# A single-core attention and two-layer feed-forward kernel: other SBUF addresses for all its tiles, the same instructions

## The chip, the cores and the metric

One Trainium2 chip, one of its cores. The metric is the device time of one execution in microseconds (us), as the median of several executions. The chip's engines are named as in the profile: PE does matmuls, PEld is PE's weight load, DVE, ACT and POOL are the vector, scalar and GpSimd engines, SP issues the transfers.

## The reference

Clustered attention, whose output goes through two feed-forward blocks. There are 2 x 8 heads of 768 positions and 64 dimensions; 1536 tokens of 512 numbers go into the blocks, each 512 to 2048 to 512.

```python
q_assign = np.argmax(np.einsum('bhsd,hcd->bhsc', q_n, c_n), axis=-1)   # q_n, k_n, c_n: normalised
k_assign = np.argmax(np.einsum('bhsd,hcd->bhsc', k_n, c_n), axis=-1)
mask = q_assign[:, :, :, None] == k_assign[:, :, None, :]
scores = np.where(mask, scale * np.matmul(q, k.transpose(0, 1, 3, 2)), -1000000000.0)
attn = np.exp(scores - np.max(scores, axis=-1, keepdims=True))
attn = attn / (np.sum(attn, axis=-1, keepdims=True) + 1e-09)
x = np.matmul(attn, v)                      # then to [tokens, heads x dims]
...
h = x @ w_in;  x = np.maximum(0.01 * h, h) @ w_out              # first block
h = x @ w_in2; r = np.maximum(h, 0.0); x = (r * r) @ w_out2     # second block
```

## The kernel before

Every fp32 operand is split into a high and a low part, and three products (high x high, high x low, low x high) stand for one fp32 product. So PE runs many matmuls on 4-byte numbers.

**Attention.** Eight pairs of heads, 48 units of two query blocks of 128 rows. A unit makes its scores on PE (`S`, line 353, 384 columns, both operands in tile `hb`), the row maximum on DVE (`nm`), the exponentials on ACT (`e`), the division on POOL, twelve transposes on PE (`T`, line 416, stationary `e`, moving the identity matrix `ident`), the split of the transposes on ACT and DVE (`eh`, `el`), and the product with V on PE (`A`, line 451, 256 columns, moving `eh` or `el`, stationary `vv`). The order of all engines is written out by hand (table PLAN).

**Feed-forward blocks.** 16 blocks of hidden units in each of the two layers, three blocks of 512 tokens: 96 units. A unit is twelve matmuls of 512 columns into `h` (line 728, stationary `wh` or `wl`, moving `xh` or `xl`) and twelve into `o` (line 770; in the first layer the weights are stationary and `gh`, `gl` move, in the second layer `gh`, `gl` are stationary and the weights move). That makes 2304 matmuls of 512 columns. The weights arrive as raw 8-byte numbers in `wraw` and are decoded by ACT, DVE and POOL (lines 131 to 160) into `wh` and `wl` while PE works on the group before.

**Where the weights lie.** Hidden blocks are worked off in groups of four (the first four in two groups of two), and the weight tiles are a ring of eight: blocks 0 to 3 of every eight lie in pool `wpx`, which is allocated from the right end of SBUF, blocks 4 to 7 in pool `wpb`, on the left. So PE works for about 66 us with weights from `wpx`, then for about 65 us with weights from `wpb`, and so on, four stretches of each.

```python
wpx = ctx.enter_context(tc.tile_pool(name="wpx", bufs=G, side="right", reuse_waits="tile"))
ring.append((ctx.enter_context(tc.tile_pool(name="wpb", bufs=RING - G, reuse_waits="tile")), RING))
pool = next(q for q, n in ring if ci % RING < n)      # ci: the hidden block's number
```

**Addresses.** Pools are laid out one after the other, those of the left side upwards behind the DMA scratch, those with `side="right"` downwards from 229344 bytes in each partition. In the built program of before:

| tile (pool) | start in its partition, bytes | past a multiple of 512 | past a multiple of 128 |
|---|---|---|---|
| `ident` (const) | 16512 | 128 | 0 |
| `xh`, `xl` (xp) | 21600, 46176 | 96 | 96 |
| `hb`, `vv`, `e`, `eh`, `el`, `gh`, `gl`, `acc` and the other large tiles of the left side | 70752 and up | 96 | 96 |
| `wh`, `wl` (wpb, left) | 99424 to 128096, in steps of 4096 | 96 | 96 |
| `wh`, `wl` (wpx, right) | 184288 to 212960, in steps of 4096 | 480 | 96 |
| `rqk`, `spl`, `rv` (right, in the attention alone) | 189408 and up | 480 | 96 |

PE's operands are slices of these tiles at multiples of 512 bytes, so a slice has its tile's remainder (the 32-column `cbd` in `S` excepted).

Of the kernel before, what the change touches and what calls it, by code (L numbers as in the profile page):

```python
# [8 lines left out]
F32 = mybir.dt.float32  # L9
# [43 lines left out]
def attention_moe_moe_kernel(  # L53
# [9 lines left out]
    nc = tc.nc  # L63
# [17 lines left out]
    WARM = (9,4,10)  # L81

    const = ctx.enter_context(tc.tile_pool(name="const", bufs=1))
    xp = ctx.enter_context(tc.tile_pool(name="xp", bufs=1))

    xh = xp.tile([128, HP, NT], F32R, name="xh")
    xl = xp.tile([128, HP, NT], F32R, name="xl")
# [590 lines left out]
    for u in range(-1, NU + 5):  # L678
# [8 lines left out]
        for op in PLAN[FIRST[u] if p == 0 else u % UPP].split():  # L687
            if ":" in op:
                name, lag = op.split(":")
# [5 lines left out]
            else:  # L695
                name, ahead = op.split("@")
# [184 lines left out]
```

## Time and profile before

| what | value |
|---|---|
| time, median of 3 executions (lowest to highest) | 786.04 us (784.79 to 786.47) |
| the profiled execution's own time from its first to its last instruction (span) | 782.9 us |
| PE busy, of the span | 770.1 us (98%), 4147 matmuls |
| DVE, ACT, POOL busy | 532.2, 410.8, 293.4 us |
| attention: S, T and A matmuls | 384, 576 and 576 |
| feed-forward: matmuls into h and into o, 512 columns each | 1152 and 1152 |
| data moved by DMA | 66.35 MB, mean 85 GB/s |

The profile takes one execution. Its span is 3.1 us less than the median of the timed executions. A matmul's duration in the profile is its latency: matmuls overlap, so the pace of PE is read from the start of one piece of work to the start of the next, not from the durations.

### The profile page before, as it was taken

Reading aid. Unit: us, or ns where it says so; the run is one execution under the profiler, and the core shown is the slowest. Engines: PE = TensorE matmul, PEld = TensorE weight load, DVE = VectorE, ACT = ScalarE, POOL = GpSimd, SP = SyncE. Lnnn points to the kernel's source line nnn. Section 1 sums busy time; section 2 is a strip of 40 time slices with the busy share of each in tenths; the row PEclk is TensorE's granted clock in tenths of the full one; section 3 lists DMA queues with packets and bytes.
Section 4 is the critical chain, followed back from the end, with each engine's and each line's share of the span. In section 5 each row is a group of like instructions: output and inputs, shape, how many; then the busy total and the mean of one; then the engine's idle time right before and its main releaser. Section 6 shows DMA issues by size and latency. Waiting matters only on the chain.

```text
span 782.9 us, 11015 instructions
## 1 busy us (share of the span) xinstructions
PE 770.1 (98%) x4147; PEld 665.3 (85%) x4147; DVE 532.2 (68%) x772; ACT 410.8 (52%) x759; POOL 293.4 (37%) x258
## 2 busy tenths in 40 slices
PE   8999999999999999999999999999999999999998
PEld 8899999999988888888888888888888888888886
DVE  5899999999998568775664577487257557533333
ACT  6988988988997563443442343445344234212121
POOL 2989889889765412221220214442022012100000
PEclk9999999999999999999999999999999999999999
DMA  7594574573502223233121113013113103000102
GB/s 224 121 205 110 105 180 108 113 164 78 139 1 93 96 85 108 105 107 108 55 107 54 33 75 108 1 54 108 55 54 108 54 0 108 1 0 1 52 17 95
DMA packets 16005, 66.35 MB, mean 85 GB/s; under 512 B 2704, under 2 KB 2704, under 8 KB 10960
## 3 DMA queue, kind: packets, MB, share of 16 engines
q1 hardware_dynamic: 15952, 65.64, 29.2%
q8 instruction: 33, 0.54, 0.3%
q14 instruction: 20, 0.16, 0.1%
HBM read 44.60 MB, written 3.15 MB: 61 GB/s over the span
## 4 chain that ended last, share of the span: by engine, by line
PE 82%; DVE 12%; ACT 4%; issue 1%; POOL 0%; DVEq 0%; ACTq 0%; POOLq 0%
PE o L770 34%; PE h L728 33%; PE A L451 5%; PE S L353 4%; DVE el L433 4%; PE T L416 4%; DVE nm L376 4%; ACT e L386 2%; DVE xt L473 1%; ACT eh L427 1%; DVE ds L279 1%; PE warm L202 1%; PE ohT L308 1%; DVE m L278 1%; PE S L257 1%
## 5 line engine op out<-in xcount | busy, mean ns | idle before, releaser
L160 POOL TENSOR_TENSOR wl<-wt,wh 128x1024 fp32r<-128x1024 f32 x32 | 77.5, 2423 | 297.1 <-ACT wh L159 246.6
L728 PE MATMUL h<-xl,wh 128*128 128x512 f32 x384 | 150.6, 392 | 0.0
L728 PE MATMUL h<-xh,wl 128*128 128x512 f32 x384 | 150.5, 392 | 0.0
L728 PE MATMUL h<-xh,wh 128*128 128x512 f32 x384 | 150.4, 393 | 0.0
L749 DVE TENSOR_TENSOR gl<-g,gh 128x512 fp32r<-128x512 f32 x96 | 91.6, 954 | 44.1 <-ACT gh L748 44.0
L748 ACT CAST gh<-g 128x512 fp32r<-128x512 f32 x96 | 59.6, 621 | 80.5 <-DVE g L745 42.2
L433 DVE TENSOR_TENSOR el<-T,eh 128x512 fp32r<-128x512 f32 x144 | 94.4, 683 | 5.6 <-ACT eh L427 3.7
L403 POOL TENSOR_SCALAR e<-e,r 128x768 f32<-128x768 f32 x96 | 88.5, 933 | 20.7 <-DVE r L400 13.4
L376 DVE TENSOR_REDUCE nm<-S 128x1 f32<-128x768 f32 x96 | 90.8, 947 | 4.6 <-PE S L257 2.3
L386 ACT ACTIVATE e<-S,nm 128x768 f32<-128x768 f32 x96 | 87.0, 906 | 11.1 <-DVE nm L376 6.8
L353 PE MATMUL S<-hb 128*128 128x384 f32 (+1 forms) x384 | 90.5, 350 | 1.6 <-ACT e L386 1.2
L745 DVE TENSOR_TENSOR g<-t 128x512 f32<-128x512 f32 x48 | 39.5, 822 | 73.3 <-ACT t L744 73.2
L744 ACT ACTIVATE t<-h 128x512 f32<-128x512 f32 x48 | 28.7, 598 | 113.3 <-PE h L728 113.2
L728 PEld LDWEIGHTS h<-xh,wl 128*128 128x128 f32 x384 | 72.3, 188 | 16.1
L728 PEld LDWEIGHTS h<-xl,wh 128*128 128x128 f32 x384 | 72.2, 188 | 16.0
L728 PEld LDWEIGHTS h<-xh,wh 128*128 128x128 f32 x384 | 72.2, 188 | 15.9
L427 ACT CAST eh<-T 128x512 fp32r<-128x512 f32 x144 | 79.4, 586 | 10.6 <-PE T L416 10.2
L451 PE MATMUL A<-eh,vv 128*128 128x256 f32 x288 | 79.5, 307 | 3.0 <-DVE xt L473 3.0
L416 PE MATMUL T<-ident,e 128*128 128x128 f32 x576 | 80.0, 274 | 1.1 <-DVE el L433 1.0
L770 PE MATMUL o<-gh,wl 128*128 128x512 f32 x192 | 75.4, 393 | 0.0
L770 PE MATMUL o<-gl,wh 128*128 128x512 f32 x192 | 75.3, 392 | 0.0
L770 PE MATMUL o<-wh,gl 128*128 128x512 f32 x192 | 75.3, 392 | 0.0
(106 smaller groups left out, 1407.0 us busy)
## 6 DMA issues: line engine op xcount, KB each, us to landing
wraw<-w SPq DMA_DIRECT2D x32, 1024.0 KB, 4.7
hb<-spl SPq DMA_DIRECT2D x14, 576.0 KB, 4.8
hb<-spl SPq DMA_DIRECT2D x42, 192.0 KB, 5.1
rqk<-qk SPq DMA_DIRECT2D x16, 384.0 KB, 4.5
rv<-v SPq DMA_DIRECT2D x8, 384.0 KB, 4.1
out<-ob SPq DMA_DIRECT2D x12, 256.0 KB, 2.1
twice<-qk SPq DMA_DIRECT2D x8, 192.0 KB, 6.0
hb<-st SPq DMA_DIRECT2D x28, 48.0 KB, 2.7
```

Of the source, the lines that this page charges most:

```text
L160: nc.gpsimd.tensor_tensor(out=wl, in0=t, in1=wh.bitcast(F32), op=ALU.subtract)
L353: nc.tensor.matmul(out=s[:, c, 0:HALF], lhsT=hb[0:k, a, i * 128 : (i + 1) * 128], rhs=hb[0:k, b, c * HALF : (c + 1) * HALF], start=(a == 0 ...
L376: nc.vector.tensor_reduce(out=n, in_=s_t[t][:, :, 0:HALF], axis=AX.XY, op=ALU.max, negate=True)
L386: nc.scalar.activation(out=e.rearrange("p (a b) -> p a b", a=2), in_=s_t.pop(t)[:, :, 0:HALF], func=AF.Exp, bias=n_t.pop(t), scale=1.0, ac ...
L403: nc.gpsimd.tensor_scalar(out=e_t[t], in0=e_t[t], scalar1=r_t[t // 2][:, t % 2 : t % 2 + 1], scalar2=1.0, op0=ALU.mult, op1=ALU.mult,)
L416: nc.tensor.transpose(T[:, o : o + 128], e_t[2 * u + b][:, kc * 128 : (kc + 1) * 128], ident)
L427: nc.scalar.copy(out=eh[:, 2 * g : 2 * g + 2, :].rearrange("p a b -> p (a b)"), in_=T_t[u, g])
L433: nc.vector.tensor_tensor(out=el[:, 2 * g : 2 * g + 2, :].rearrange("p a b -> p (a b)"), in0=T_t.pop((u, g)), in1=eh[:, 2 * g : 2 * g + 2, ...
L451: nc.tensor.matmul(out=A, lhsT=w, rhs=m[:, kc, :], start=(kc == 0 and i == 0), stop=(kc == KC - 1 and i == 1),)
L728: nc.tensor.matmul(out=h, lhsT=w[:, ws], rhs=x[:, kk, c], start=(kk == 0 and i == 0), stop=(kk == HP - 1 and i == 2),)
L749: nc.vector.tensor_tensor(out=gl, in0=g, in1=gh.bitcast(F32), op=ALU.subtract)
L770: nc.tensor.matmul(out=outs[o], lhsT=l, rhs=r, start=(first and i == 0), stop=(last and i == 2),)
```

## The change

Three edits. The scratch that is set aside for DMA at the bottom of SBUF takes 4096 bytes in each partition instead of 16384. A tile of 928 bytes that nothing reads or writes stands first in the pool `const`. A tile of 2016 bytes that nothing reads or writes stands first on the right side.

```diff
     const = ctx.enter_context(tc.tile_pool(name="const", bufs=1))
+    const.tile([128, 232], F32, name="cpad")
     xp = ctx.enter_context(tc.tile_pool(name="xp", bufs=1))
+    rpad = ctx.enter_context(tc.tile_pool(name="rpad", bufs=1, side="right"))
+    rpad.tile([128, 504], F32, name="rp")
...
-    nc = bacc.Bacc("TRN2", target_bir_lowering=False, num_devices=1)
+    nc = bacc.Bacc("TRN2", target_bir_lowering=False, num_devices=1, dynamic_dma_scratch_size=4096)
```

In the built program each engine has the same instructions in the same order with the same waits; only source line numbers and tile numbers differ. What differs is the addresses. Every tile of the left side lies 11360 bytes lower (12288 less, 928 more), every tile of the right side 2016 bytes lower:

| tile (pool) | start now | past a multiple of 512 | past a multiple of 128 |
|---|---|---|---|
| `ident` (const) | 5152 | 32 | 32 |
| `xh`, `xl` (xp) | 10240, 34816 | 0 | 0 |
| the other large tiles of the left side | 59392 and up | 0 | 0 |
| `wh`, `wl` (wpb, left) | 88064 to 116736 | 0 | 0 |
| `wh`, `wl` (wpx, right) | 182272 to 210944 | 0 | 0 |
| `rqk`, `spl`, `rv` (right) | 187392 and up | 0 | 0 |

Two tiles of one side keep their distance. A tile of the right side and one of the left side are now a multiple of 512 apart; before they were 384 bytes past one.

## Rows read from the trace of the kernel before

**Rows 1.** The page: busy us, share and instructions of each engine; then 40 slices.
```profile
PE 770.1 (98%) x4147; PEld 665.3 (85%) x4147; DVE 532.2 (68%) x772; ACT 410.8 (52%) x759; POOL 293.4 (37%) x258
...
PEclk9999999999999999999999999999999999999999
```

**Rows 2.** Windows: stretch in us, its length, busy time and instructions of each engine.
```profile
8.00:248.00 240.00, 233.31 (x1787) 224.44 (x1786) 221.75 (x391) 210.40 (x462) 193.30 (x182) 1.00 0.52 124
...
385.00:445.00 60.00, 60.00 (x260) 48.67 (x260) 33.66 (x45) 20.59 (x29) 7.21 (x3) 1.00 0.15 53
459.00:503.00 44.00, 44.00 (x195) 36.45 (x195) 27.45 (x31) 18.69 (x29) 17.04 (x10) 1.00 0.20 72
```

**Rows 3.** Chain that ended last, 350 to 364 us (wpb): start, us, what.
```profile
352.15 2.72 PE o L770 x12
354.87 2.72 PE h L728 x12
357.59 2.72 PE o L770 x12
360.31 2.72 PE h L728 x12
```

**Rows 4.** The same view, 421 to 433 us (wpx, first layer).
```profile
421.21 2.79 PE h L728 x12
424.00 2.78 PE o L770 x12
426.78 2.79 PE h L728 x12
429.57 2.79 PE o L770 x12
```

**Rows 5.** The same view in the second layer: 528 to 543 us (wpx).
```profile
528.53 2.78 PE o L770 x12
...
539.66 2.78 PE o L770 x12
```

**Rows 6.** The same view in the second layer: 619 to 640 us (wpb).
```profile
619.62 2.72 PE h L728 x12
622.34 2.72 PE o L770 x12
```

**Rows 7.** Groups by line over the span: busy us, mean ns, idle us before.
```profile
L728 PE MATMUL h<-xl,wh 128*128 128x512 f32 x384 | 150.6, 392 | 0.0
...
L770 PE MATMUL o<-gh,wl 128*128 128x512 f32 x192 | 75.4, 393 | 0.0
```

**Rows 8.** Chain that ended last, 140 to 150 us (attention).
```profile
144.33 0.88 PE T L416 x8
...
147.20 0.96 PE A L451 x8
148.16 0.71 PE S L353 x4
```

**Rows 9.** Groups by line: PE from 778.7 us on, PE's last matmuls.
```profile
L770 PE MATMUL o<-wl,gh 128*128 128x512 f32 x1 | 0.4, 390 | 0.0
...
L770 PE MATMUL o<-wh,gl 128*128 128x512 f32 x1 | 0.4, 388 | 0.0
```

**Rows 10.** Page, DMA queues (packets, MB, share) and issues (us to landing).
```profile
q1 hardware_dynamic: 15952, 65.64, 29.2%
...
wraw<-w SPq DMA_DIRECT2D x32, 1024.0 KB, 4.7
...
hb<-spl SPq DMA_DIRECT2D x42, 192.0 KB, 5.1
```

**Rows 11.** Waits by engine: us in total, times, longest us.
```profile
ACT wt L131 <- DMA wraw<-w: 28.4, 12, 4.2
...
PE S L353 <- ACT e L386: 1.2, 1, 1.2
```

## The prediction

> **What bounds the kernel now.** The page's busy times come first: PE is busy for 770.1 of 782.9 us, and the granted clock is at its upper level, 2.4 GHz, in all 40 slices [rows 1]. That leaves 12.8 us of PE's idle time to win by any reordering, so what counts is how long PE takes for one matmul. The windows then show two stages. From 8 to 248 us, the attention, PE is busy for 233.31 of 240 us, but DVE for 221.75 and ACT for 210.40 as well; in the feed-forward blocks PE never stops (60.00 of 60, 44.00 of 44) and DVE has half its time free [rows 2]. The groups by line say the same: no idle time at all before the matmuls of lines 728 and 770 [rows 7].
>
> Then the pace, which is the point of this case. The chain of waits in the feed-forward blocks is PE alone, in pieces of twelve matmuls. In a stretch whose weights lie in wpb, four pieces follow each other from 352.15 to 363.03 us: 48 matmuls in 10.88 us, 226.7 ns each [rows 3]. In a stretch with weights from wpx, four pieces take from 421.21 to 432.36 us: 11.15 us, 232.3 ns each [rows 4]. The second layer repeats it: 2.78 against 2.72 us for twelve [rows 5, 6]. The instructions, shapes, clock and other engines' kinds of work are the same in both stretches, and PE waits for nothing in either. What differs is where the weights lie, and both matmul lines are slow there, whether the weights are the stationary operand (line 728, and line 770 in the first layer) or the moving one (line 770 in the second). So the place of an operand in SBUF already costs PE 5.6 ns a matmul in half of the feed-forward work. The built program says how the two places differ: 96 bytes past a multiple of 512 for wpb as for xh, xl, gh and gl, 480 past one for wpx; and wpx lies some 70 KB higher.
>
> **The change, part by part.**
>
> The weights of wpx. Blocks 0 to 3 of every eight are half of the 96 units, so 48 x 24 = 1152 matmuls. They come to lie as wpb lies against xh and gh, a whole multiple of 512 apart. If the start is what slows them, each goes from 232.3 to 226.7 ns: 1152 x 5.6 ns = 6.5 us less. The bounds: nothing, if the height and not the start makes the difference; 6.5 us, plus what the next paragraph may add. I take the whole 6.5, since the trace has one cleanly good pace and the move gives these operands the relation that goes with it.
>
> The start at 0 instead of 96 for everything else. 512 columns at 2.4 GHz are 213.3 ns, so the good pace still has 13.3 ns on top [rows 3]. PE's last matmul has no weight load behind it and still takes 388 ns, like its neighbour's 390 [rows 9], so the extra is the matmul's own and not the load beside it. In the attention A takes 0.96 us for 8 (120 ns for 256 columns, 13.3 on top) and S 0.71 for 4 (177.5 for 384, 17.5 on top) [rows 8]. All of these have operands 96 bytes past a multiple of 128. Whether 0 takes anything off that, no row shows. The bounds are nothing and all of it: 2304 x 13.3 ns = 30.6 us in the feed-forward blocks. In the attention it would be 384 x 17.5 + 576 x 13.3 = 14.4 us on PE, of which little can show, as DVE is nearly as busy there. I take nothing, because 13.3 ns can as well be a fixed cost of a matmul with its own weight load, which every one of these is.
>
> The identity matrix. It moves from a multiple of 128 to 32 bytes past one, the only operand that gets a less even start. T takes 0.88 us for 8, 110 ns each [rows 8], for 128 columns that need 53.3 ns. The bounds: nothing, and the 10 ns by which A's 120 exceeds it, 576 x 10 ns = 5.8 us. I take nothing: T is twice as long as its columns need, which leaves room for a late first column.
>
> The smaller DMA scratch. Nearly all packets go through queue q1, hardware_dynamic, issued by SP [rows 10]; no instruction names the scratch. Weights land in 4.7 us and ACT waits 28.4 us in all for them, while PE waits for no transfer (its wait before S is for ACT, 1.2 us) [rows 10, 11]. Cost: nothing; the cover is PE's own work, and without it those 28.4 us would be the upper end.
>
> DVE, ACT and POOL do the same work on the same shapes at starts that are multiples of 32 before and after: nothing is taken. When PE is 5.6 ns faster per matmul, a wpx stretch shrinks by 1.6 us; DVE is busy for 33.66 of 60 us there [rows 2], so the decoding of the next weights stays hidden and no new wait follows.
>
> The sum: 782.9 - 6.5 = 776.4 us of span. The median of the timed runs is 3.1 us above the profiled span, so 779.5 us.
>
> Two rules are weighed against this. The Trainium skill (SBUF — State Buffer, Specifications) speaks of lines of 16 bytes and asks no more than two hits in each; 96 and 480 are both multiples of 16, so by it no start in this kernel should be better than another, and the sum would be zero, 786.0. The 5.6 ns between the stretches don't fit that rule unless they come from something else. In the other direction the skill (TensorE: Matmul & The Clock Gate, Back-to-back issue gap) gives N/2.4 + 2.5 ns between matmuls, 215.8 ns for 512 columns; if an even start led there, the sum would be an estimated 2304 x 10.9 ns + 6.5 us = 31.6 us less, about 754. No row here shows that pace.
>
> **The rivals.**
>
> *The even start takes off the extra too.* If all 13.3 ns go, the feed-forward blocks lose 30.6 + 6.5 = 37.1 us and the time is 749; if half go, 21.8 us and 764. For it: the extra is the matmul's own [rows 9], addresses demonstrably matter, and all slow-by-13 operands share the uneven start. Against it: the extra isn't one number (13.3, 13.3, 17.5), and no matmul of this kind with an even start stands in the trace. Chance 0.25.
>
> *Nothing happens.* The place matters by its height, or by which half of SBUF it is in, and wpx stays where it is but for 2016 bytes: 786.0. For it: start and height change together between the two stretches, so the trace can't part them. Against it: the pieces of S, with both operands low on the left, have 17.5 ns on top, so low tiles aren't always at the good pace. Chance 0.19, with those mixtures in which a gain of the weights and a loss at T cancel.
>
> *Slower: 0 is a bad start.* 480 and 0 are 32 bytes apart, 96 is on the other side; if a slice that begins within 32 bytes of a multiple of 512 is the slow kind, the matmuls of the wpb stretches lose what those of wpx lose now, 1152 x 5.6 ns = 6.5 us, and those of wpx win nothing: 792.5. For it: one of only two starts that the trace shows is slow, and 0 is the neighbour of that one. Against it: starts on even boundaries cross the fewest of them. It decides as soon as twelve matmuls of a wpb stretch take over 2.72 us. Chance 0.14.
>
> **How the numbers follow.** The forecast case has a chance of 0.42, its own range 778 to 782. With 0.25 for the deeper gain it makes faster 0.66, since a small part of the forecast case may fall within 0.2% (1.6 us, about what a measurement of this kernel can tell from no change); same is 0.20, slower 0.14. The range takes in the forecast, the deeper gain down to its full price, and no change with its spread: 749 to 788. It leaves out the slower case.
>
> **What would show it.** In the chain of waits, pieces of twelve at 2.72 us in the stretches that now have 2.78 and 2.79, and 2.72 unchanged in the others: forecast. All pieces well under 2.72: the deeper gain, with S under 0.71 for 4. 2.79 where it is now: the height. 2.79 everywhere: 0 is bad. T above 0.88 for 8 would show the identity matrix. An idle time before line 728 or 770, or a landing time of wraw above 4.7 us, would mean that the scratch or the decoding matters after all, and the sum is wrong in a term that I set to nothing.

## The result and the profile after

The median is 778.3 us (777.93 to 778.99, 4 executions), against 785.79 us (784.79 to 786.47, 4 executions) for the kernel before in the same comparison. The ratio is 0.9911, 95% interval 0.9897 to 0.9925: faster, by 0.9%. The profiled execution took 777.93 us and has a span of 776.1 us, where 776.4 was forecast.

In the kernel after, all source lines below the fillers are three higher: `h` is line 731, `o` line 773, `S` 356, `T` 419, `A` 454.

The chain of waits of the kernel after, 421 to 433 us, a stretch with weights from wpx (start in us, length in us, what), the counterpart of [rows 4]:

```profile
421.55 2.72 PE o L773 x12
424.26 2.72 PE h L731 x12
426.99 2.72 PE o L773 x12
```

The same view in the second layer, 528 to 543 us, again wpx, beside [rows 5]:

```profile
530.35 2.72 PE o L773 x12
533.07 2.72 PE h L731 x12
535.79 2.72 PE o L773 x12
```

And 350 to 364 us, weights from wpb, beside [rows 3]:

```profile
350.83 2.72 PE o L773 x12
353.55 2.72 PE h L731 x12
```

The two kinds of stretches have become one. What was 2.78 and 2.79 is 2.72; what was 2.72 has stayed 2.72, though every operand in it now starts at a multiple of 512 instead of 96 past one. The groups by line of the kernel after give the same in sums: the mean latency fell from 392 and 393 ns [rows 7] to 389.

```profile
L731 PE MATMUL h<-xl,wh 128*128 128x512 f32 x384 | 149.5, 389 | 0.0
...
L773 PE MATMUL o<-gh,wl 128*128 128x512 f32 x192 | 74.8, 389 | 0.0
```

In the attention nothing has moved. The chain of waits of the kernel after, 140 to 150 us, beside [rows 8]:

```profile
144.56 0.88 PE T L419 x8
...
147.43 0.95 PE A L454 x8
148.39 0.71 PE S L356 x4
```

The chain also dates the gain. The first long piece of feed-forward matmuls begins at 251.17 us before and at 251.41 after, so the attention brought nothing. The last piece of work on DVE begins at 779.21 us before and at 772.46 after. The whole gain, 7.0 us, lies between. The rows are of the chain of waits, first of the kernel before, then of the one after:

```profile
251.17 5.12 PE h L728 x22
...
779.21 0.69 DVE ob L797
```

```profile
251.41 5.02 PE h L731 x22
...
772.46 0.69 DVE ob L800
```

### The profile page after: what moved, and what is told of

Read it like the earlier page. It is cut to its first block, busy times and chain, and to the rows that moved or that the text cites. A ratio compares the mean times of both kernels' runs of the same rounds, so it can differ in the third digit from the quotient of the medians.

```text
span 776.1 us, 11015 instructions
## 1 busy us (share of the span) xinstructions
PE 763.0 (98%) x4147; PEld 665.0 (86%) x4147; DVE 532.5 (69%) x772; ACT 410.0 (53%) x759; POOL 293.4 (38%) x258
## 4 chain that ended last, share of the span: by engine, by line
PE 82%; DVE 11%; ACT 5%; issue 1%; POOL 0%; DVEq 0%; ACTq 0%; POOLq 0%
PE o L773 34%; PE h L731 33%; PE A L454 5%; PE S L356 4%; PE T L419 4%; DVE el L436 4%; DVE nm L379 3%; ACT e L389 3%; ACT eh L430 1%; DVE xt L476 1%; DVE ds L282 1%; PE warm L205 1%; PE ohT L311 1%; DVE m L281 1%; PE S L260 1%
## 5 line engine op out<-in xcount | busy, mean ns | idle before, releaser
L773 PE MATMUL o<-wl,gh 128*128 128x512 f32 x192 | 74.8, 390 | 0.0
L773 PE MATMUL o<-wh,gh 128*128 128x512 f32 x192 | 74.8, 390 | 0.0
```

The source lines that it names most:

```text
L773: nc.tensor.matmul(out=outs[o], lhsT=l, rhs=r, start=(first and i == 0), stop=(last and i == 2),)
```

## The experiments

Three theories could still explain the two paces. Theory D: what counts is the distance between the two operands of a matmul, the one that moves and the weights, and a multiple of 512 (or of some smaller number) is good. Theory S: each operand's own start counts, and 480 past a multiple of 512 is a bad one. Theory H: the high end of SBUF is slow. The change itself can't part D from S, since it put both right at once.

**One side at a time.** Against the kernel before, the filler of the right side alone:

```diff
+    rpad = ctx.enter_context(tc.tile_pool(name="rpad", bufs=1, side="right"))
+    rpad.tile([128, 504], F32, name="rp")
```

> Only the 2016-byte filler of the right side; the scratch and the left side as before. The weights of wpx now start at a multiple of 512, the left side stays 96 past one. Theory D (what counts is the distance between the two operands of a matmul, a multiple of 512 being good): the distance is 416, not a multiple, so the wpx stretches stay near 2.79 us for twelve matmuls and the time near 786. Theory S (what counts is each operand's own start; 480 past a multiple of 512 is bad, 0 and 96 are good): all pieces 2.72, span about 776, time about 778 to 779. Theory H (the height in SBUF): 786.

Measured: 786.71 us, ratio 1.0014 (1.0005 to 1.0023). Its chain of waits at 421 to 433 us, wpx:

```profile
422.84 2.80 PE h L730 x12
425.64 2.80 PE o L772 x12
428.44 2.80 PE h L730 x12
```

The weights lie at multiples of 512, as they do in the change, and the pace is 233 ns. An even start of the weights is worth nothing by itself: theory S fails here.

The left side alone, with the smaller scratch:

```diff
+    const.tile([128, 232], F32, name="cpad")
...
-    nc = bacc.Bacc("TRN2", target_bir_lowering=False, num_devices=1)
+    nc = bacc.Bacc("TRN2", target_bir_lowering=False, num_devices=1, dynamic_dma_scratch_size=4096)
```

> The smaller scratch and the 928-byte filler of the left side; the right side as before, 480 past a multiple of 512, the left side at multiples of it. Theory D: the distance is 480, no multiple of 512, so the wpx stretches stay slow, about 786 (how slow a distance of 480 is nobody has seen: 2.75 to 2.85 us for twelve). Theory S: the weights of wpx keep their bad start, 786. Should it be as fast as the change, both are wrong and something on the left side did it.

Measured: 785.52 us, ratio 1.0003 (0.9994 to 1.0012). Its chain of waits at 421 to 433 us, wpx:

```profile
421.22 2.80 PE h L729 x12
424.02 2.80 PE o L771 x12
```

So neither half of the change gains anything alone. The gain belongs to the pair.

**All starts equally uneven.** The kernel before with one filler on the left, so that both sides are 480 past a multiple of 512:

```diff
+    const.tile([128, 96], F32, name="cpad")
```

> The scratch and the right side of before, and a filler of 384 bytes on the left, so that every large tile of both sides is 480 past a multiple of 512. Theory D: the distance is a multiple of 512 everywhere, so all pieces are 2.72 us and the time is 778 to 779. Theory S: all operands have the bad start, all pieces 2.78 or more, 792 or more. This and the filler of the right side alone part the two theories in opposite directions.

Measured: 778.26 us, ratio 0.9908 (0.9895 to 0.9922). The chain of waits at 421 to 433 us, wpx:

```profile
422.26 2.72 PE o L771 x12
424.98 2.72 PE h L729 x12
427.70 2.72 PE o L771 x12
```

Here no large tile has an even start, all have the one that theory S called bad, and the kernel is as fast as the change. With the last two runs this settles it between S and D: the distance between the operands counts, not the start of either.

**The scratch.** The change with the scratch of before:

```diff
-    nc = bacc.Bacc("TRN2", target_bir_lowering=False, num_devices=1, dynamic_dma_scratch_size=4096)
+    nc = bacc.Bacc("TRN2", target_bir_lowering=False, num_devices=1)
```

> Both fillers, but the scratch of before, 16384 bytes: all large tiles start at multiples of 512 as in the change, 12288 bytes higher on the left. Theories D and S: as the change, 2.72 us for twelve everywhere, 778 to 779. If the smaller scratch itself brought anything, the time is above that of the change by it.

Measured: 778.03 us, ratio 0.9909 (0.9896 to 0.9923). The size of the scratch is worth nothing either way; in the change it is only 12288 bytes, a multiple of 512, by which the left side moved.

**Which distances are good.** Four kernels, all from the change, in which the weight tiles of wpx are 128 bytes longer. The four blocks in the pool then have four different distances (here: the start of the weights less the start of the other operand, past a multiple of 512), and a smaller filler of the right side shifts all four. The edit (the filler is 504, 496, 488 and 480 numbers long in the four):

```diff
+            more = 32 if pool is ring[0][0] else 0
-            wh = pool.tile([128, 2 * DM], F32R, tag="wh", name="wh")
-            wl = pool.tile([128, 2 * DM], F32R, tag="wl", name="wl")
+            wh = pool.tile([128, 2 * DM + more], F32R, tag="wh", name="wh")[:, 0 : 2 * DM]
+            wl = pool.tile([128, 2 * DM + more], F32R, tag="wl", name="wl")[:, 0 : 2 * DM]
```

> The change, but the weight tiles of wpx are 4224 bytes long instead of 4096, so that the four pairs of wh and wl lie 0, 384, 256 and 128 bytes past a multiple of 512 while everything else is at multiples of it. If a multiple of 512 is needed: one block of four (distance 0) at 2.72 us for twelve, the three others at 2.75 or more, a span of about 776 + 4.9 = 781. If a multiple of 256 is enough: two blocks of four good, about 779. If some distance is better than 0, its pieces fall under 2.72.

> As the last, all 32 bytes further: distances 32, 416, 288 and 160. If a multiple of 512 (or 256) is needed exactly, all four blocks are slow, a span of about 782 to 783. If near is enough, the block at 32 is better than the others.

> As the last, distances 64, 448, 320 and 192. If the distance must be a multiple of 512 or 256: all four blocks slow, a span of about 782 to 783. If a multiple of 64 were enough, all good, 776; the 384 of the kernel before speaks against that.

> As the last, distances 96, 480, 352 and 224. All four blocks slow if the distance must be a multiple of 512 or 256, a span of about 782 to 783; 480 should repeat the pace of the left fillers alone, 2.78 to 2.79 us for twelve.

One execution each: spans of 781.9, 783.9, 782.8 and 785.2 us, times of 783.64, 785.75, 784.56 and 786.95. The paces are in the chains of waits. The first, from 399 us on; by the program's order its pieces belong to the blocks at 0, 256, 384 and 128, one after the other:

```profile
399.61 2.73 PE h L732 x12
402.34 2.73 PE o L774 x12
405.06 2.79 PE h L732 x12
407.85 2.80 PE o L774 x12
```

The second, from 402 us on, in the same way 288, 416 and 160, and further on 32:

```profile
402.13 2.80 PE o L774 x12
404.93 2.80 PE h L732 x12
407.73 2.80 PE o L774 x12
...
421.73 2.80 PE h L732 x12
```

The third, from 402 us on, 320, 448 and 192, and further on 64:

```profile
402.29 2.80 PE o L774 x12
405.09 2.76 PE h L732 x12
407.85 2.75 PE o L774 x12
...
421.68 2.80 PE h L732 x12
```

The fourth, from 400 us on, 96, 352, 480 and 224:

```profile
400.49 2.81 PE h L732 x12
403.30 2.81 PE o L774 x12
406.11 2.80 PE h L732 x12
408.90 2.80 PE o L774 x12
```

So 256 is as good as 0; 192 and 448, which are 64 short of a multiple of 256, are half as bad as the rest in this first layer; all other distances that were seen cost the full 6 ns or so, and none is better than 0. A distance of 32 is among the bad ones: near isn't enough.

It also matters which of the two operands moves. In the second layer the weights are the moving operand of `o` and the stationary one of `h`. There the block at 448 of the third kernel takes the full price in `o` and half of it in `h` (the first and second row), and the block at 64 takes half of it in `o`, where it runs in pieces of six (the third row):

```profile
528.68 2.79 PE o L774 x12
...
537.08 2.75 PE h L732 x12
...
546.58 1.38 PE o L774 x6
```

The span of the first kernel, 781.9 us, is nearer to the 781 expected for one good block than to the 779 for two, though two are good. In part that is because its feed-forward matmuls begin 1.1 us later than those of the change (at 242.80 and 241.67 us), and because its good pieces take 2.73 us and not 2.72. The paces, not the spans, tell good from bad here.

**The smallest filler that does it.** If a multiple of 256 is all that is needed, 128 bytes on the right side of the kernel before will do:

```diff
+    rpad = ctx.enter_context(tc.tile_pool(name="rpad", bufs=1, side="right"))
+    rpad.tile([128, 32], F32, name="rp")
```

> The kernel before with one filler of 128 bytes on the right side and nothing else: the weights of wpx come to lie 256 bytes past a multiple of 512 from xh, gh and gl. If a distance of 256 is as good as one of 512, as the scan has it for one block of four: 2.72 us for twelve everywhere, a time as that of the change, 778 to 779. If only multiples of 512 are good: 2.75 or more in the wpx stretches, 783 or more.

Measured: 777.81 us, ratio 0.9909 (0.9894 to 0.9924). Its chain of waits at 421 to 433 us, wpx:

```profile
422.92 2.72 PE o L772 x12
425.64 2.72 PE h L730 x12
```

One filler of 128 bytes gives what the whole change gives, with all starts 96 past a multiple of 256. It isn't faster than the change: the intervals cover each other.

**The other pool.** The change with a filler of 128 bytes ahead of wpb:

```diff
+    off = ctx.enter_context(tc.tile_pool(name="off", bufs=1, reuse_waits="tile"))
+    off.tile([128, 32], F32, name="off")
     ring.append((ctx.enter_context(tc.tile_pool(name="wpb", ...
```

> The change with a filler of 128 bytes ahead of the left weight pool, so that the weights of wpb lie 128 bytes past a multiple of 256 from xh, gh and gl, and those of wpx stay at a multiple. Theory D: the two kinds of stretches change places, 2.78 to 2.79 us for twelve with wpb, 2.72 with wpx, about 785. Theory H (the high end of SBUF is what is slow): the wpb stretches stay at 2.72, 778.

Measured: 785.96 us, ratio 1.0009 (0.9999 to 1.0018). Its chain of waits, 350 to 364 us (wpb) and 421 to 433 us (wpx):

```profile
352.25 2.79 PE o L775 x12
355.04 2.79 PE h L733 x12
...
421.15 2.72 PE h L733 x12
423.87 2.72 PE o L775 x12
```

The two kinds of stretches have changed places. The low pool is as slow at a bad distance as the high one was, and theory H falls.

## Why the prediction was right, point by point

The weights of wpx: right in mechanism and size. The term was 1152 x 5.6 ns = 6.5 us; the span fell by 6.8 us, from 782.9 to 776.1. It had left open whether start, relation or height decides; the filler of the right side alone and the kernel with 480 everywhere say that it is the relation, and wpb at a bad distance says that it isn't the height. So the term's condition, that the start is what slows these matmuls, was wrong, and its other reason, the relation, was right. The forecast held all the same because the change put start and relation right at once, and not because the prediction knew which of them it was: to that extent it was luck. (wpx lies 84864 bytes above wpb, not some 70 KB.) The rest of the 7.0 us in the feed-forward blocks fits the groups' borders, where units of both pools alternate: before, a piece of a wpb unit between two of wpx took 2.76 us there (the chain of waits of the kernel before, 366 to 392 us; the pieces of `o` belong to wpb, those of `h` to wpx). So the slow pace reached a little into its neighbours, which the term left out.

```profile
379.43 2.76 PE o L770 x12
382.19 2.80 PE h L728 x12
384.99 2.76 PE o L770 x12
387.74 3.25 PE h L728 x14
```

The start at 0 for everything else: right at nothing. Pieces of twelve stay at 2.72 us, S at 0.71 for 4, A at 0.95 for 8. The 13.3 ns on top of 512 columns are there at starts of 0, 96 and 480 alike, as long as the distance is good. The rival of a deeper gain, which had a chance of 0.25, is out: the start doesn't make this part. What does make it stays open. That it is the matmul's own, and not the load beside it, as the prediction read it, isn't shown either: 388 and 390 ns [rows 9] are latencies, which say nothing of the pace.

The identity matrix: nothing, as taken. T is 0.88 us for 8, with `ident` now 32 past a multiple of 128. By what the runs showed since, this tested little: `ident` and `e` lie on the same side, `ident` 32 past a multiple of 512 from `e` in every kernel here, before and after. For the matmuls of 512 columns, 32 either way was a slow distance; whether T would gain at a multiple of 256, no run tried. The scratch: nothing, as taken; the run with the old scratch has the same ratio. ACT's wait for raw weights is 30.5 us after and was 28.4 before [rows 11], and PE still never waits in the feed-forward blocks.

The step from span to time was a little off, and is why 778.3 was measured and not 779.5. The 3.1 us between the profiled span of before and the median weren't a fixed part: the profiled execution of after took 777.93 us with a span of 776.1, 1.8 us more. In the runs beside the first experiments, an execution of the kernel before with a span of 782.9 us took 784.73 us, again 1.8 us more. So 782.9 was the span of one of its faster executions, and the 3.1 us set it against the median of all. With 1.8 the forecast would have been 778.2.

The rival that nothing happens rested on height, which wpb at a bad distance rules out. The prediction's argument against it, from S, which has 17.5 ns on top though it lies low, is still unexplained: S kept its 0.71 us, and both its operands in `hb` lie a multiple of 512 apart in every kernel here.

The slower rival, that 0 is a bad start, is out: with 0 everywhere all pieces are at 2.72 us.

Of the two rules, the one on lines of 16 bytes (the Trainium skill, SBUF — State Buffer, Specifications) would have all these kernels alike, as every start and distance here is a multiple of 16; this case's traces don't agree, with 226.7 ns at a distance of 0 or 256 and 232 to 234 at most others. The one of N/2.4 + 2.5 ns (the Trainium skill, TensorE: Matmul & The Clock Gate, Back-to-back issue gap) gives 215.8 ns for 512 columns, and the section calls that the gap of a matmul by itself, not of a stream of weight loads and matmuls as here. No distance and no start tried here came under 226.7 by more than the noise of a piece, so for these matmuls of 4-byte numbers with a weight load each the measurement decides.

## What to carry to other kernels

Where PE never waits, compare its pace between stretches of equal matmuls before looking for idle time: here the slow and the fast half of the same work stood side by side in the chain of waits. When they differ with the pool, look at the distance in bytes between the moving operand and the weights; in this kernel it had to be a multiple of 256, and one filler of 128 bytes was enough. Aligning the other large tiles did nothing beyond that.

## What the runs showed of the hardware

A matmul of 512 columns of 4-byte numbers was issued every 226.7 ns when its two operands lay a multiple of 256 bytes apart within a partition, and every 229 to 235 ns otherwise, at a granted clock of 1.00 (2.4 GHz), whichever of the two pools was at the bad distance. The weight load of the next matmul begins within about 5 ns of the start of the running one in all of them. The timeline of the kernel after (start, length, engine, line) shows it at a good distance:

```profile
530.18 0.39 PE L773 MATMUL o<-wh,gh 128*128 128x512 f32 x1
530.19 0.19 PEld L773 LDWEIGHTS o<-wl,gh 128*128 128x128 f32 x1
530.41 0.39 PE L773 MATMUL o<-wl,gh 128*128 128x512 f32 x1
```

So two reads of SBUF run side by side, and that they get into each other's way at most distances is a natural reading. The traces bear it out in part, at places where blocks of the two pools meet (starts from the trace, addresses from the built program). In the kernel before, 14 matmuls whose own operands are at a good distance are followed by one whose weights lie 384 past a multiple of 512 from the operand still moving. They take 232.5 ns from start to start, against 227.1 where the next weights are at a good distance too. In the kernel with the one filler of 128 bytes, where that 384 is 256, the same 14 take 227.1. Four others are followed by a matmul that is at a bad distance itself, but whose weights are at a good one from the operand still moving: 226.8. So the load of the next weights takes part. That it is the whole cause isn't shown: the same kind of place at 320 and 352 in the third and fourth kernels with longer tiles takes 226.0 and 228.2 (six matmuls each), and behind a slow stretch the first seven or so matmuls at a good distance are still slow, which makes the 2.76 us above. Why a multiple of 256 is good stays open.
